# Converting the first two w_out tiles into a pool that opens with the second half of the attention

## The chip, the cores and the metric

The kernel runs on one core of a Trainium2 chip. The metric is the device time of one execution in microseconds (us); three executions of the kernel before took 803.8, 806.29 and 808.18 us, so the median is 806.29 us.

## What is computed

Attention for 4 batches, 8 heads, 576 positions and 64 dimensions, with a bias from a small network of relative positions, and behind it an MLP with a squared ReLU on the 2304 tokens:

```python
def _attn_ref(q, k, v, w1, b1, w2):
    ...
    h = np.maximum(x @ w1 + b1, 0.0)
    bias = h @ w2
    scores = scores + bias.transpose(2, 0, 1)[None, :, :, :]
    scores = scores - np.max(scores, axis=-1, keepdims=True)
    attn = np.exp(scores)
    attn = attn / (np.sum(attn, axis=-1, keepdims=True) + 1e-09)
    return np.matmul(attn, v).astype(np.float32)

def _moe_ref(x, w_in, w_out):       # x: 2304 x 512, w_in: 512 x 2048, w_out: 2048 x 512
    h = x @ w_in
    r = np.maximum(h, 0.0)
    g = r * r
    return (g @ w_out).astype(np.float32)
```

## The kernel before, in words

**Stages.** The attention runs in 80 units (batch, pair of heads, chunk of 128 rows), numbered `s` in the loop at L615; the second half, of batches 2 and 3, begins at `s == NA` = 40. There the pool `pre` opens on the left side of SBUF (L620). The MLP comes behind it: it runs over `items` (L684), each one block of tokens `n` and one pair `P` of 128-wide slices of the hidden layer. `up(i)` (L691) makes the products with w_in: 24 matmuls into the PSUM tile `ha`, 18 into `hb` (L704), then scales and combines them on ACT (L718), POOL (L719, L720) and DVE (L722, L723), squares them, and splits the result into a high part `gh` (ACT, L733) and a low part `gl` (DVE, L734). `down(i)` (L737) makes 24 matmuls with w_out (L753), for the item before. There is one `ha` and one `hb`, so the next item's `hb` matmuls wait until L722 and L723 have read the last ones.

**Weights.** Both weight matrices arrive as 64-bit floats and are cut into 32 tiles; tile `n` belongs to w_out where `n // 2` is odd (2, 3, 6, 7, 10, ...). A tile is loaded by one 512 KB transfer on SP into a buffer of the tag `stage` (L172), of which there are two. `lead_w` (L175) puts the 32-bit float together: one pass on ACT (L180) and four on DVE (L183 to L186). For w_out, `split_out` (L242) then writes the high part on ACT (L246) and the low part on POOL (L247) into the tile that the matmuls read. For w_in, `split_in` adds sums on POOL (L238 to L240) and ends with L227 on ACT and L228 on DVE. "A conversion" below is all of this for one tile. The scratch tile `wa` of a w_out conversion has two buffers, and each is free only when L247 has run.

**Order of the work.** Tiles of w_in up to 21 are converted during the attention, one in every second unit (`early`, `when`, L611 to L613). The remaining 20 tiles are in the list `todo` (L790); `convert(k)` takes the next `k` of them, with two loads ahead. `convert(C0)` takes two before the first item, and `convert(WC[i])` (L824) takes `WC[i]` between `up(i)` and `down(i - 1)`. A scheduler in the framework then sets the order on each engine from its own model of times, so instructions of the MLP can stand among those of the attention if their data and memory allow it. The tiles that the matmuls of w_out read lie in the pool `mlp` on the right side, in the place where the pools `att` and `kqb` of the attention were; `pre` holds `stage`, `wa` and `zw`.

**Stage buffers at item 3.** The outputs of `down(3)` are partial sums: each of four tiles `o` takes a `stage` buffer (L759), is copied from PSUM by ACT (L769) or DVE (L767), and is stored to DRAM (L772). They take their turn in the same two buffers as the weight loads.

Of the kernel before, what the change touches and what calls it, by code (L numbers as in the profile page):

```python
# [11 lines left out]
F32R = mybir.dt.float32r  # L12
# [23 lines left out]
WB, WS, LW, XS, XB, LAG, NE, SC, SN, AH = 40, 3, 4, 48, 70, 1, 13, 22, 16, 2  # L36
# [9 lines left out]
LW = 2  # L46
# [33 lines left out]
def attention_then_relu2_mlp(ctx: ExitStack, tc: tile.TileContext, q, k, v, cols, w_in, w_out, psi, xmat, dist, out):  # L80
# [47 lines left out]
    NU = len(units)  # L128
# [6 lines left out]
    def load_k(b, hp):  # L135
        t = kq_p[-1].tile([128, KO], F32, name="k1", tag="k1")
        SP.dma_start(out=t[0:64, :S], in_=k[b, hp, :, :S])
        SP.dma_start(out=t[64:128], in_=k[b, hp, :, S:])
        k1_t[b, hp] = t

    def load_v(b, hp):
        t = att.tile([128, 5, 2, D], F32, name="v", tag="v", bufs=AB * HP)
        SP.dma_start(out=t, in_=v[b, hp])
        v_t[b, hp] = t

    def load_q(b, hp):
        t = kq_p[-1].tile([128, S], F32, name="q1", tag="q1")
        for h in range(2):
            rows = slice(64 * h, 64 * h + 64)
            SP.dma_start(out=t[rows, 512:], in_=q[b, hp, TAIL, :, h, rows])  # L150
            SP.dma_start(out=t[rows, :512].rearrange("d (i m) -> d i m", i=TAIL), in_=q[b, hp, :TAIL, :, h].rearrange("i d m -> d i m"))
        q_t[b, hp] = t
# [16 lines left out]
    def load_w(n):  # L169
        t = stage_p["p"].tile([128, 2, 256, 2], I32, name="stage", tag="stage", bufs=2)  # L170
        src = (w_in, w_out)[n // 2 % 2][n // 4 * 2 + n % 2]
        SP.dma_start(out=t.rearrange("p g n t -> p g (n t)"), in_=src.bitcast(I32).rearrange("p (g n) -> p g n", g=2))  # L172
        wraw_t[n] = t

    def lead_w(n, a):  # L175

        raw = wraw_t.pop(n)
        low, high = (raw[:, :, :, t] for t in range(2))
        af = a.bitcast(F32)
        ins = ACT.activation(out=af, in_=high.bitcast(F32), func=AF.Abs)  # L180
        if n in early:
            tc.keep_in_program_order(ins)
        DVE.tensor_scalar(out=af, in0=af, scalar1=HI_MIN, scalar2=HI_MAX, op0=ALU.max, op1=ALU.min)  # L183
        DVE.tensor_scalar(out=a, in0=a, scalar1=3, scalar2=0x3FFFFFFF, op0=ALU.logical_shift_left, op1=ALU.bitwise_and)
        DVE.scalar_tensor_tensor(out=a, in0=high, scalar=-0x40000000, in1=a, op0=ALU.bitwise_and, op1=ALU.bitwise_or)  # L185
        DVE.scalar_tensor_tensor(out=a.bitcast(U32), in0=low.bitcast(U32), scalar=29, in1=a.bitcast(U32), op0=ALU.logical_shift_right, op1=ALU.bitwise_or)  # L186
# [21 lines left out]
    def scan_w(k):  # L208
        tc.keep_in_program_order(largest(wraw_t.pop(ins[k])[:, :, :, 1].bitcast(F32), wcols[:, k:k + 1]))

    def scale_w(ps_col):
        m = column()
        mi = m.bitcast(I32)
        largest(wcols, m)
        DVE.tensor_scalar(out=m, in0=m, scalar1=HI_MIN, scalar2=HI_MAX, op0=ALU.max, op1=ALU.min)
        t = column()
        DVE.tensor_scalar(out=t.bitcast(I32), in0=mi, scalar1=3, scalar2=0x3FFFFFFF, op0=ALU.logical_shift_left, op1=ALU.bitwise_and)
        DVE.scalar_tensor_tensor(out=mi, in0=mi, scalar=0x40000000, in1=t.bitcast(I32), op0=ALU.bitwise_and, op1=ALU.bitwise_or)
        return power(m, ps_col)

    def split_in(n, dst):
        z = stage_p["p"].tile([128, 9, 128], F32, name="zw", tag="zw")
        lead_w(n, z[:, 0:4].rearrange("p (g a) b -> p g (a b)", g=2).bitcast(I32))
        left_sums(z)
        hi, lo = dst
        sig = wscale[0]
        ACT.activation(out=hi, in_=z[:, 2:9], func=AF.Identity, scale=sig)  # L227
        DVE.scalar_tensor_tensor(out=lo, in0=z[:, 2:9], scalar=sig, in1=hi, op0=ALU.mult, op1=ALU.subtract)  # L228
        w_t[n] = (hi, lo)
# [5 lines left out]
    def left_sums(z):  # L235

        tt = POOL.tensor_tensor
        tt(out=z[:, 4:6], in0=z[:, 0:2], in1=z[:, 2:4], op=ALU.subtract)  # L238
        tt(out=z[:, 6:8], in0=z[:, 1:3], in1=z[:, 2:4], op=ALU.add)
        tt(out=z[:, 8], in0=z[:, 0], in1=z[:, 3], op=ALU.add)  # L240

    def split_out(n, dst):  # L242
        a = stage_p["p"].tile([128, 2, 256], F32, name="wa", tag="wa", bufs=2)
        lead_w(n, a.bitcast(I32))
        hi, lo = (x.rearrange("p (g n) -> p g n", g=2) for x in dst)
        ACT.copy(hi, a)  # L246
        POOL.tensor_tensor(out=lo, in0=a, in1=hi.bitcast(F32), op=ALU.subtract)  # L247
        w_t[n] = dst

    def is_in(n):  # L250
        return n // 2 % 2 == 0
# [277 lines left out]
    todo = [(ic, jb) for ic in chunks for jb in range(NJB)]  # L529
# [32 lines left out]
    wdst, xsig, alpha_t = {}, {}, {}  # L562
# [3 lines left out]
    def take(x, o, n):  # L566
        o += 18 * S * x
        return area[:, o:o + n]

    NB, NP = B + 1, NF // 2  # L570
# [13 lines left out]
    for m in range(1, 8):  # L584
        t = take(1, 896 + 512 * (m - 1), 512).bitcast(F16).rearrange("p (x c t) -> p x c t", x=2, c=2)
# [25 lines left out]
    for m, n in enumerate(early):  # L611
        last = (896 * m + 895) // (9 * S) if m < 11 else 2
        when[n] = max(WB + WS * m, NA + (B - AB) * NIC * (last + 1))  # L613
    waiting = []
    for s in range(NU + TL + 1):  # L615
        if s == NA:
            prep_stack.close()
            kq_stack.close()
            kq_p.append(kq_stack.enter_context(tc.tile_pool(name="kqb", bufs=3, side="right", reuse_waits="tile")))
            pre = ctx.enter_context(tc.tile_pool(name="pre", bufs=1, side="left", reuse_waits="tile"))  # L620
            stage_p["p"] = pre
            xT.extend(pre.tile([128, HP, S], F32, name=f"xT{b}") for b in range(AB, B))
        for m, g in enumerate(groups[AB * HP:]):
            if s == max(first[g] - KL, NA):
                load_k(*g)
                load_q(*g)
            if s == max(first[g] - KL + TL + 1, NA - AB * HP + 2 + TL + m):
                load_v(*g)
        if s == SC - 1:
            load_w(ins[0])  # L630
            load_w(ins[1])
        for n in early:
            if when[n] == s + LW:
                load_w(n)
        if s < NU:
            scores(s)
        if SC <= s < SC + SN:
            for m in range(NF * (s - SC) // SN, NF * (s - SC + 1) // SN):
                scan_w(m)
                if m + 2 < NF:  # L640
                    load_w(ins[m + 2])
        if s == SC + SN:
            pw = ps.tile([128, 512], F32, name="pw", tag="aux", bufs=4)
            wscale = scale_w(pw[:, 0:1])
        for n in early:
            if when[n] == s:
                split_in(n, wdst[n])
        if s == XS:
            pw = ps.tile([128, 512], F32, name="pw", tag="aux", bufs=4)
            set_scale(0, x_largest(0), pw[:, 0:1])  # L650
        if s == XB:
            split_x(0)
        if s < AB * HP * TAIL:
            n, r = divmod(s, AB * HP)
            bias_upto(NJB * (n + 1) + BO[r])
            if r == 4 and n + 2 < NIC:
                load_xc(chunks[n + 2])
        if 0 <= s - TL < NU:
            transposes(s - TL)
        if 0 <= s - TL - 1 < NU:  # L660
            values(s - TL - 1)
            b, hp, ic = units[s - TL - 1]
            if s - TL - 1 == NU - 1 or units[s - TL][:2] != (b, hp) and (b >= AB or ic == chunks[-1]):
                waiting.append((b, hp, normalise(b, hp)))
            elif waiting:
                scale_x(*waiting.pop(0))
        while waiting and s == NU + TL:
            scale_x(*waiting.pop(0))
# [108 lines left out]
                SP.dma_start(out=tails, in_=o)  # L777

    for n in range(4 * NP):
        if not is_in(n) and n < 4 * NP - 2:  # L780
            t = mlp.tile([128, 2, 512], F32R, name=f"w{n}")
            wdst[n] = (t[:, 0], t[:, 1])

# [6 lines left out]
    todo = [4 * P + 2 + f for P in range(NP // 2) for f in range(2)]  # L790
    for P in range(NP // 2, NP):
        todo += [n for n in range(4 * P, 4 * P + 4) if n not in early]
    done = loaded = 0
    def convert(k):
        nonlocal done, loaded
# [12 lines left out]
    for i in range(len(items) + LAG):  # L808
        if i == NP // 2:
            tmp_stack.close()  # L810
            late = ctx.enter_context(tc.tile_pool(name="late", bufs=1, side="right", reuse_waits="tile"))
            for n in (4 * NP - 2, 4 * NP - 1):
                t = late.tile([128, 2, 512], F32R, name=f"w{n}")
                wdst[n] = (t[:, 0], t[:, 1])
        if i < len(items):
            n, P = items[i]
# [60 lines left out]
```

## Time and profile before

| what | value |
|---|---|
| median of three executions | 806.29 us (803.8 to 808.18) |
| profiled execution, its time | 803.41 us |
| its span, first to last instruction | 801.6 us |
| granted TensorE clock, mean | 0.967 |
| busy PE, DVE, ACT, POOL | 731.9, 546.0, 453.8, 272.8 us |
| attention | 0 to about 402 us |
| MLP | about 402 us to the end |

The span leaves out what lies before the first and behind the last instruction (1.8 us here). Engines named: PE does matmuls, ACT, DVE and POOL work on vectors, SP issues the transfers. Times of rows are us from the start of the span, and `[2.16 <-DVE xT L723]` in a row says that the engine was idle for 2.16 us before it, and what ended that. [...]

### The profile page before, as it was taken

How to read it: one execution, taken by the hardware profiler on the slowest of the kernel's cores; microseconds unless marked ns; L12 is line 12 of the kernel's file. 1: busy time of each engine (PE TensorE's matmuls, PEld its weight loads, DVE VectorE, ACT ScalarE, POOL GpSimd, SP SyncE). 2: the span in 40 equal slices, each digit the busy share in tenths (PEclk: the TensorE clock that was granted, in tenths of full speed). 3: DMA queues.
4: the chain of work that ended last, by engine and by line, in shares of the span. 5: the costliest groups of instructions: out<-in, count | busy, mean ns of one | idle time of the engine just before them, and what ended most of it. 6: DMA issues, size and time to landing. Idle time of an engine off the chain costs nothing.

```text
span 801.6 us, 17870 instructions
## 1 busy us (share of the span) xinstructions
PE 731.9 (91%) x7238; PEld 583.4 (73%) x7238; DVE 546.0 (68%) x1135; ACT 453.8 (57%) x924; POOL 272.8 (34%) x292
## 2 busy tenths in 40 slices
PE   6499999999988898988999899989999999999992
PEld 5457787777766676666678677767888888888881
DVE  7877888875457778887888968785654466445541
ACT  5767787777645468786865555575642233224320
POOL 1454323340001012141266645745451244223320
PEclk7979999999999999999999999999999999999997
DMA  7610000000475422211221132102020001000100
GB/s 207 188 57 17 3 16 3 2 3 5 125 276 196 159 81 88 84 54 54 80 90 70 66 119 104 55 1 79 1 79 1 1 1 54 1 1 2 53 2 26
DMA packets 27990, 50.14 MB, mean 63 GB/s; under 512 B 5252, under 2 KB 13444, under 8 KB 27908
## 3 DMA queue, kind: packets, MB, share of 16 engines
q1 hardware_dynamic: 27908, 49.01, 18.6%
q8 instruction: 57, 0.93, 0.5%
q14 instruction: 25, 0.20, 0.1%
HBM read 43.23 MB, written 5.77 MB: 61 GB/s over the span
## 4 chain that ended last, share of the span: by engine, by line
PE 53%; DVE 17%; ACT 8%; DMA 7%; issue 7%; POOL 4%; SPq 2%; POOLq 0%; DVEq 0%; ACTq 0%
PE y L753 16%; PE sp L428 8%; PE px L495 7%; PE ha L704 7%; PE hb L704 6%; PE pp L477 5%; DMA stage<-in_w_in 4%; PE bb L383 4%; DVE t L434 2%; ACT p L439 2%; DVE area L605 2%; ACT pt L478 1%; DVE zw L185 1%; DVE area L228 1%; DVE small L189 1%
## 5 line engine op out<-in xcount | busy, mean ns | idle before, releaser
L753 PE MATMUL y<-w,gh 128*128 128x512 f32 x576 | 176.7, 401 | 2.6 <-ACT gh L733 2.4
L704 PEld LDWEIGHTS <-area 128*128 128x128 f16 x1680 | 148.1, 99 | 42.2 <-issue 17.6
L439 ACT ACTIVATE p<-t,negm 128x576 f32<-128x576 f32 x144 | 111.4, 776 | 27.3 <-DVE negm L434 27.1
L434 DVE CUSTOM_DVE_ANT_0 t<-sp,area 128x576 f32<-128x576 f32 x144 | 104.0, 753 | 29.9 <-PE sp L428 24.8
L753 PEld LDWEIGHTS y<-w,gh 128*128 128x128 f32 x576 | 105.1, 190 | 23.9 <-ACT gh L733 3.8
L428 PE MATMUL sp<-k,q 64*128 64x288 f32 (+1 forms) x640 | 105.3, 441 | 15.4 <-DVE negm L434 7.6
L495 PE MATMUL px<-pt,v 128*64 128x128 f32 (+1 forms) x1600 | 99.2, 272 | 7.5 <-DVE xT L500 2.8
L753 PE MATMUL y<-w,gl 128*128 128x512 f32 x288 | 106.0, 395 | 0.0
L704 PE MATMUL ha<-area 128*128 128x256 f16 (+1 forms) x960 | 105.2, 263 | 0.5 <-DVE xT L466 0.5
L478 ACT COPY pt<-pp 128x512 f32<-128x512 f32 x144 | 80.4, 583 | 41.5 <-PE pp L477 41.4
L495 PEld LDWEIGHTS px<-pt,v 128*64 128x64 f32 x1600 | 81.5, 139 | 24.2 <-issue 9.5
L704 PE MATMUL hb<-area 128*128 128x256 f16 (+1 forms) x720 | 83.9, 270 | 8.0 <-DVE area L723 4.7
L477 PE MATMUL pp<-ident,p 128*128 128x128 f32 x576 | 84.7, 283 | 3.3 <-ACT p L439 2.5
L428 PEld LDWEIGHTS sp<-k,q 64*128 64x128 f32 (+1 forms) x640 | 55.2, 179 | 39.7 <-issue 14.0
L398 POOL TENSOR_TENSOR area<-bt,bt 128x256 f32<-128x256 f32 x72 | 53.5, 768 | 80.6 <-DVE bt L393 80.6
L477 PEld LDWEIGHTS pp<-ident,p 128*128 128x128 f32 x576 | 62.2, 142 | 21.3 <-issue 8.4
L383 PE MATMUL bb<-wmov,mask 128*128 128x64 f16 x1440 | 51.2, 197 | 13.7 <-DVE bt L404 11.0
L753 PEld LDWEIGHTS y<-w,gl 128*128 128x128 f32 x288 | 53.7, 188 | 11.9 <-DVE gl L734 0.7
L383 PEld LDWEIGHTS <-mask 128*128 128x128 f16 x1440 | 46.9, 100 | 20.7 <-DVE bt L404 11.8
L719 POOL TENSOR_TENSOR area<-area 128x512 f32<-128x512 f32 (+1 forms) x20 | 24.3, 1215 | 92.8 <-ACT area L718 83.9
L369 DVE TENSOR_TENSOR mask<-sdist,theta 128x1024 f16<-128x1024 f16 (+1 forms) x78 | 50.3, 677 | 7.9 <-PE bb L383 7.9
L733 ACT CAST gh<-area 128x512 fp32r<-128x512 f32 (+1 forms) x40 | 22.2, 574 | 44.0 <-DVE area L728 32.9
(146 smaller groups left out, 1024.2 us busy)
## 6 DMA issues: line engine op xcount, KB each, us to landing
stage<-in_w_in SPq DMA_DIRECT2D x32, 512.0 KB, 3.7
stage<-in_w_out SPq DMA_DIRECT2D x16, 512.0 KB, 3.5
v<-in_v SPq DMA_DIRECT2D x16, 320.0 KB, 3.7
out<-o SPq DMA_DIRECT2D x18, 256.0 KB, 2.0
q<-in_q SPq DMA_DIRECT2D x32, 128.0 KB, 2.9
k<-in_k SPq DMA_DIRECT2D x16, 160.0 KB, 3.5
k<-in_k SPq DMA_DIRECT2D x16, 144.0 KB, 3.5
xc<-in_xmat SPq DMA_DIRECT2D x5, 288.0 KB, 3.3
```

The costliest lines, as they stand in the source:

```text
L369: DVE.tensor_tensor(out=m[:, :, :w], in0=win, in1=th.to_broadcast([128, 8, w]), op=ALU.is_ge)
L383: PE.matmul(bb[:, 64 * (7 - r):64 * (8 - r)], lhsT=m[:, r], rhs=wmov[:, n], start=(n == 0), stop=(n == 1))
L398: POOL.tensor_tensor(out=dst, in0=tw, in1=sw, op=ALU.add)
L428: mm = PE.matmul(out_t[to, x, :HALF], lhsT=qt[rows, cols], rhs=kt[rows, k0:k0 + HALF], start=True, stop=True)
L434: DVE.tensor_tensor_reduce(out=t.rearrange("p (x n) -> p x n", x=2), in0=sp[:, :, :HALF], in1=bias.rearrange("p (x n) -> p x n", x=2), sca ...
L439: ACT.activation(out=p[:, S * n:S * n + S], in_=t, func=AF.Exp, bias=negm[:, n:n + 1], scale=-1.0, accum_out=sums[:, 2 * ic + n:2 * ic + n ...
L477: PE.transpose(pp[:, 128 * c:128 * c + 128], p[:, k0:k0 + 128], ident)
L478: ACT.copy(pt[:, 4 * h:4 * h + 4], pp.rearrange("p (c m) -> p c m", c=4))
L495: PE.matmul(px[64 * h:64 * h + 64, :w], lhsT=vt[:, c, h], rhs=src, start=(c == 0), stop=(c == 4))
L704: PE.matmul(h[:, s, :w], lhsT=a, rhs=x, start=(k == 0), stop=(k == 5))
L719: POOL.tensor_tensor(out=c[:, 2:4], in0=s[:, 1:3], in1=s[:, 0:4:3], op=ALU.subtract)
L753: PE.matmul(y, lhsT=a[:, slot, o:o + 128], rhs=x, start=((n, P) in firsts and f == 0 and m == 0), stop=((n, P) in lasts and f == 1 and m = ...
```

## The change

Tiles 2 and 3, the first two of w_out, get their destination in `pre` instead of `mlp`, and their loads and conversions are written into the loop over the attention's units: the loads at `s` = 75 and 77, the conversions at 77 and 79. They leave `todo`, so that `convert` begins with tile 6, and every later tile comes two places earlier in it; `C0` and `WC` stay.

```diff
@@ attention loop
+    first_out = {2: NU - 3, 3: NU - 1}
...
             stage_p["p"] = pre
+
+            for n in first_out:
+                t = pre.tile([128, 2, 512], F32R, name=f"w{n}")
+                wdst[n] = (t[:, 0], t[:, 1])
...
             if when[n] == s:
                 split_in(n, wdst[n])
+        for n, at in first_out.items():
+            if s == at - LW:
+                load_w(n)
+            if s == at:
+                split_out(n, wdst[n])
@@ MLP
-        if not is_in(n) and n < 4 * NP - 2:
+        if not is_in(n) and n < 4 * NP - 2 and n not in first_out:
             t = mlp.tile([128, 2, 512], F32R, name=f"w{n}")
...
+    todo = [n for n in todo if n not in first_out]
```

How the order of the instructions moves is shown at three places. Lines of the changed kernel are 10 higher in `up` and `down` (L722 is L732, L723 is L733, L734 is L744, L718 is L728, L767 is L777), and 0 in the helpers ahead of the attention loop.

**First place: ACT at the end of the attention.** `w` is the converted tile, `wa` its scratch, `pt` and `pp` the transposed probabilities, `zw` the scratch of a w_in tile. Before:

```order
L227 ACTIVATE area<-zw,small 128x896
L478 COPY pt<-pp 128x512
L481 COPY pt<-pa 128x128
L246 CAST w_6235<-wa 128x512
L246 CAST w_6236<-wa 128x512
L180 ACTIVATE wa<-stage 128x512 x2
L718 ACTIVATE s<-ha,small 128x1024
```

With the change:

```order
L227 ACTIVATE area<-zw,small 128x896
L180 ACTIVATE wa<-stage 128x512
L478 COPY pt<-pp 128x512
L481 COPY pt<-pa 128x128
L246 CAST w_4001<-wa 128x512
L180 ACTIVATE wa<-stage 128x512
L246 CAST w_6257<-wa 128x512
L180 ACTIVATE wa<-stage 128x512
L728 ACTIVATE s<-ha,small 128x1024
```

The L246 of tile 2 has gone 12 rows up, to right behind the L180 of the last w_in tile; tile 6's L180 now stands ahead of the last L478, and tile 10's L180 ahead of the first item's L728.

**Second place: DVE from the last L228 of the attention to the first item.** Up to this L228 the order on DVE is the same in both. `ra` and `rt` are the last sums of the attention, `xT` its output. Before:

```order
L228 SCALAR_TENSOR_TENSOR area<-zw,small,area 128x896
L500 COPY xT_4001<-px 128x128
L500 COPY xT_4001<-px 128x64
L466 TENSOR_TENSOR xT_4001<-xT_4001,ra 128x512
L466 TENSOR_TENSOR xT_4001<-xT_4001,rt 128x64
L189 TENSOR_REDUCE small<-xT_4001 128x1 x2
L189 TENSOR_REDUCE small<-small 128x1 x2
```

With the change:

```order
L228 SCALAR_TENSOR_TENSOR area<-zw,small,area 128x896
L183 TENSOR_SCALAR wa<-wa 128x512
L500 COPY xT_4003<-px 128x128
L184 TENSOR_SCALAR wa<-wa 128x512
L185 SCALAR_TENSOR_TENSOR wa<-stage,wa 128x512
L500 COPY xT_4003<-px 128x64
L186 SCALAR_TENSOR_TENSOR wa<-stage,wa 128x512
L466 TENSOR_TENSOR xT_4003<-xT_4003,ra 128x512
L466 TENSOR_TENSOR xT_4003<-xT_4003,rt 128x64
```

The four passes of tile 6 have moved ahead of L466. Behind them, the passes of tiles 7 and 10 both end ahead of the first L732 and L733; before, tiles 6 and 7 were there, and the last pass of tile 7 stood between the two.

**Third place: DVE at the end of item 4.** `gl` is the low part for `down(3)`; `xT` is here the scratch of item 4, and the `o` is the first of the two output tiles of item 3 that DVE copies. Before, the two L722 and L723 follow the passes of tile 18:

```order
L734 TENSOR_TENSOR gl<-area,gh 128x512
L605 SCALAR_TENSOR_TENSOR area<-area,small 128x512
L185 SCALAR_TENSOR_TENSOR wa<-stage,wa 128x512
L186 SCALAR_TENSOR_TENSOR wa<-stage,wa 128x512
L722 SCALAR_TENSOR_TENSOR xT_77<-hb,small,xT_77 128x2x256
L723 SCALAR_TENSOR_TENSOR xT_77<-hb,small,xT_77 128x2x256
```

With the change:

```order
L185 SCALAR_TENSOR_TENSOR wa<-stage,wa 128x512
L186 SCALAR_TENSOR_TENSOR wa<-stage,wa 128x512
L183 TENSOR_SCALAR wa<-wa 128x512
L184 TENSOR_SCALAR wa<-wa 128x512
L185 SCALAR_TENSOR_TENSOR wa<-stage,wa 128x512
L186 SCALAR_TENSOR_TENSOR wa<-stage,wa 128x512
L732 SCALAR_TENSOR_TENSOR xT_77<-hb,small,xT_77 128x2x256
L733 SCALAR_TENSOR_TENSOR xT_77<-hb,small,xT_77 128x2x256
L183 TENSOR_SCALAR zw<-zw 128x512
L184 TENSOR_SCALAR zw<-zw 128x512
L777 COPY o<-y_6449 128x512
L185 SCALAR_TENSOR_TENSOR zw<-stage,zw 128x512
```

A third conversion (tile 23, behind tiles 19 and 22) has come in between the split of the next block's tokens (L605) and item 4's L732, and the copy to `o` stands inside the conversion of tile 24. From there on the conversions run about one item ahead: none is left among the L605 of the next split, where before tiles 30 and 31 stood.

## Rows read from the trace of the kernel before

**Rows 1.** The page: busy tenths of PE in 40 slices of 20 us.

```profile
PE   6499999999988898988999899989999999999992
```

**Rows 2.** Busy time by stretch: stretch, its length, busy us of each engine, PEclk, DMA.

```profile
450.00:460.00 10.00, 7.98 (x60) 6.23 (x57) 9.79 (x10) 6.86 (x10) 7.88 (x6) 1.00 0.18 58
460.00:470.00 10.00, 7.92 (x44) 5.69 (x43) 7.33 (x10) 6.18 (x8) 4.16 (x3) 0.83 0.30 97
...
530.00:540.00 10.00, 7.34 (x48) 5.55 (x47) 9.97 (x13) 4.62 (x7) 5.10 (x4) 0.86 0.00 0
540.00:801.60 261.60, 246.51 (x1744) 204.65 (x1741) 127.63 (x192) 87.69 (x135) 88.69 (x78) 0.98 0.07 23
```

**Rows 3.** Order of time, PE, 445 to 545: start, us, engine, line, what, [idle].

```profile
452.88 2.14 PE L704 MATMUL hb<-area 128*128 128x256 f16 x18
459.59 0.73 PE L753 MATMUL y<-w,gh 128*128 128x512 f32 x2 [1.96 <-ACT gh L733]
462.41 3.66 PE L704 MATMUL hb<-area 128*128 128x256 f16 x18 [2.08 <-DVE area L723]
...
502.02 3.03 PE L704 MATMUL hb<-area 128*128 128x256 f16 x18 [2.16 <-DVE xT L723]
513.87 2.13 PE L704 MATMUL hb<-area 128*128 128x256 f16 x18
524.01 2.13 PE L704 MATMUL hb<-area 128*128 128x256 f16 x18
536.92 3.73 PE L704 MATMUL hb<-area 128*128 128x256 f16 x18 [2.66 <-DVE area L723]
```

**Rows 4.** Single lines, whole span: DVE passes of w_out conversions, ns min/median/max.

```profile
L183 DVE TENSOR_SCALAR wa<-wa x16: 411/429/1509, 388.2 to 534.6; 128x512 f32<-128x512 f32 x16
...
L184 DVE TENSOR_SCALAR wa<-wa x16: 415/427/1403, 388.7 to 537.3; 128x512 int32<-128x512 int32 x16
...
L185 DVE SCALAR_TENSOR_TENSOR wa<-stage,wa x16: 675/692/1799, 389.2 to 538.3; 128x512 int32<-128x512 int32 x16
...
L186 DVE SCALAR_TENSOR_TENSOR wa<-stage,wa x16: 673/689/1662, 391.0 to 539.0; 128x512 uint32<-128x512 uint32 x16
```

**Rows 5.** Order of time, SP: loads of tiles 2 and 6.

```profile
382.98 0.33 SPq L172 DMA_DIRECT2D stage<-in_w_out  x1
...
395.95 0.33 SPq L172 DMA_DIRECT2D stage<-in_w_out  x1
```

**Rows 6.** Order of time, all engines, end of the attention and first items.

```profile
399.82 1.15 DVE L228 SCALAR_TENSOR_TENSOR area<-zw,small,area 128x896 f16<-128x896 f32 x1
...
399.95 1.18 ACT L246 CAST w<-wa 128x512 fp32r<-128x512 f32 x2
...
402.13 0.67 ACT L180 ACTIVATE wa<-stage 128x512 f32<-128x512 f32 x1 [1.01 <-POOL w L247]
...
402.54 0.21 DVE L466 TENSOR_TENSOR xT<-xT,rt 128x64 f32<-128x64 f32 x1
...
402.68 2.78 PE L704 MATMUL ha<-area 128*128 128x256 f16 x24 [0.51 <-DVE xT L466]
...
410.10 0.74 DVE L723 SCALAR_TENSOR_TENSOR c<-hb,small,c 128x512 f32<-128x512 f32 x1
```

**Rows 7.** Order of time, DVE at item 4.

```profile
452.07 0.75 DVE L723 SCALAR_TENSOR_TENSOR xT<-hb,small,xT 128x512 f32<-128x512 f32 x1
452.74 1.32 DVE L183 TENSOR_SCALAR wa<-wa 128x512 f32<-128x512 f32 x1
...
457.19 0.69 DVE L186 SCALAR_TENSOR_TENSOR wa<-stage,wa 128x512 uint32<-128x512 uint32 x1
```

**Rows 8.** Chain that ended last, in order of time: stores of item 3's outputs.

```profile
465.62 2.35 DMA py<-o
...
468.37 4.21 DMA py<-o
```

**Rows 9.** The page: issues, us to landing.

```profile
stage<-in_w_out SPq DMA_DIRECT2D x16, 512.0 KB, 3.5
```

## The prediction

> **What bounds the kernel now.** I read the page first: PE is busy for 9 tenths or more in most slices, and from slice 28 on in all but the last [rows 1]. So PE's work sets the time, and the question for any edit is where PE stands still. The view of busy time by stretch answers it [rows 2]: from 540 us to the end PE works 246.5 of 261.6 us, and most of the rest is the tail behind the last matmul. Between 450 and 540 there are stretches of 10 us in which it works 7.3 to 8.0, and there DVE is busy for up to 9.97. [...] The order of time on PE shows the places [rows 3]. Three times the 18 `hb` matmuls wait for a DVE instruction, L723, of the item before (2.08, 2.16 and 2.66 us), once the `y` matmuls wait for ACT (1.96 us). Behind such a stop the same 18 matmuls take 3.66, 3.03 and 3.73 us where they otherwise take 2.13.
>
> What it costs is read from the same rows. Two undisturbed `hb` groups start 513.87 and 524.01, so an item takes 10.14 us. From item 5's `hb` (452.88) to item 12's (536.92) there are 7 items in 84.04 us, where 7 x 10.14 = 71.0 would do: 13.1 us lost. Item 12's slow group adds 3.73 - 2.13 = 1.6. Together **14.7 us** can be had from this region, no more. What holds L723 back is DVE's fixed order: weight conversions stand ahead of it, one of them four passes of 2.24 us by the medians (429 + 427 + 692 + 689 ns), 2.2 by the smallest and 6.4 by the largest values [rows 4].
>
> **The change, part by part.**
>
> *What moves at all.* No instruction is added or removed. The loads of tiles 2 and 3 stand where they stood on SP: tile 2's was issued at 382.98, inside the attention, already in the kernel before [rows 5], and their DVE passes have kept their places too. What was late was the last step: both L246 ran at 399.95, since their destination lay in the attention's memory, and tile 6's L180, whose load was issued at 395.95, came only at 402.13, after a wait for a `wa` buffer that L247 had to free [rows 5, 6]. With a destination in `pre`, tile 2's L246 and L247 can run at about 392, so tile 6 starts some 2.5 us earlier, and by the order everything behind it moves forward: one conversion more is done by item 0, three more by item 4, and none is left in the split ahead of item 12.
>
> *The attention.* Tile 2's L246 (0.6 us on ACT) now stands ahead of an L478 that PE's transposed data pass through. PE has the next scores to do meanwhile, and the scores wait for DVE anyway; I cost it at nothing. Without this cover it would be 0.6 us. POOL's L247 goes into a gap in which POOL waited for DVE, with nothing queued behind it.
>
> *The start of the MLP.* DVE's last L228 ends at 399.82 + 1.15 = 400.97. Now tile 6's passes follow before L466, which releases the first `ha` matmul (402.68, behind L466's end at 402.75 by the modelled times) [rows 6]. That is 2.2 us more. Tile 10's load waits for tile 6's buffer, free at about 403.8, and lands 3.5 us later [rows 9]; its passes come behind tile 7's, from about 408.5 to 410.7, and L722 and L723 add 1.5: 412.2, against 410.10 + 0.74 = 410.84 before. So item 1 is late by **+1.5 us**. The ends: 0, if the passes fit into the wait for PE's last sums, and 3.7, if all 2.2 stays and the stop lowers the clock as at 462 (3.66 - 2.13 = 1.5).
>
> *Item 4.* Before, L723 ended at 452.82 and `hb` started at 452.88 [rows 3, 7]: no slack at all. A third conversion now stands ahead of it. Its price lies between 2.2 and 6.4 us [rows 4]; the nearest row is the next conversion at this very place, which took from 452.74 to 457.88, 5.1 us [rows 7]. I take 3.7, halfway from the median to that, since in it three passes of four were slow. DVE and PE are both late by the start's 1.5, so all of it becomes a stop, and I add 1.5 for the clock: **+5.2 us**, ends 2.2 and 7.9.
>
> *The outputs of item 3.* DVE's copy to the second `o` now stands inside tile 24's conversion, and by the buffers' turn it must wait until the first `o` is stored; the last copy waits for the second store. A store took 2.35 us, and 4.21 where the chain waited for the last [rows 8]. L722, L723 of item 5 and item 4's `gl` are queued behind. On SP the loads of tiles 23 and 24 now stand ahead of the four stores; tile 24's waits for tile 22's last pass, which is done before the first `o` is copied, so it holds none of them up. PE has `hb`, `ha` and half of `y` to do meanwhile, some 6 us. I take **+2.0**, ends 0 and 4.2.
>
> *Items 6 to 8.* Tiles 25 and 26 load only when those stores are done, as tiles 23 and 24 did before, and tile 25's passes stand ahead of a `gl`. I take **+1.0**, ends 0 and one load's 3.5 [rows 9].
>
> *What goes.* The stops at 459.59, 462.41 and 502.02 belong to pairs of conversions ahead of L722 that are now done earlier; the one at 536.92 belonged to tiles 30 and 31 among the passes of the split, and nothing of them is left there. I count all 14.7 us as gone, and what comes late instead as the four terms above. From 540 us on the two orders do the same work with PE full: nothing.
>
> *Sum:* -14.7 + 1.5 + 5.2 + 2.0 + 1.0 = **-5.0 us**. Against the profiled execution's 803.4 that is 798.4. The median of the runs is 2.9 above that execution, and I give the time against it: 806.3 - 5.0 = **801.3 us**. With all terms at their low ends it is -14.7 + 2.2 = -12.5 (793.8), at their high ends -14.7 + 19.3 = +4.6 (810.9).
>
> [...] The passes of one form take 675 to 1799 ns [rows 4], and at item 4 they are slow one after the other [rows 7] while POOL works. [...]
>
> **The rivals.**
>
> *Stops only change place* (no change). For it: DVE and POOL do the same work in 402 to 540, DVE was busy 9.79 and 9.97 of 10 us at two of the stops [rows 2], and a third conversion stands where there was no slack. Against it: the last conversions leave the split, where no new work takes their place. If the new terms reach 14 instead of 9.7, it ends at 805.6.
>
> *The change does not do what it says* (no change). The loads and the passes were in the attention before; one L246 and one L247 move, and the rest is the scheduler's order. Then the gain is one conversion's share of one stop, 2.2 us: 804.1. Against it: the order itself has moved by one item from item 4 on.
>
> *Every stop goes* (faster by more). If POOL happens to be quiet at item 4 and the stores land in 2.35 us, only 2.2 us comes back: 793.8. Against it: no conversion in this place took under 5 us.
>
> [...]
>
> **How the numbers follow.** About 0.5% of the median, 4 us, is what a measurement of this kernel can tell from no change. The forecast (801.3) gets 0.42, every stop gone 0.10: faster 0.52. Stops in other places get 0.18 and the change that does little 0.15: same 0.33. The slower rival gets 0.15. The range runs from 795 to 810: the bounds of the unknown terms, less the far ends of the first and last case, which leaves under 2 in 10 outside. The forecast's own case spans 798 to 802.3.
>
> **What would show it.** Right: no `hb` wait near item 12 and 10.1 us an item from about item 9 on; the first `ha` near 404.8; a stop of 3 to 5 us on L733 (L723 before) ahead of item 5's `hb`; DVE idle ahead of its copies to `o`, ended by a store. Wrong: tile 2's L246 still near 400, item 5's `hb` without a stop, or stops of over 2 us ahead of items 7 to 9, which I cost at 1 us in all. If the stretch from the first `ha` to item 12's `hb` is not shorter than 134.2 us, the forecast has failed.

## The result and the profile after: slower by 0.9%

The changed kernel takes 813.49 us (median of 12 executions, 809.27 to 816.44) against 806.28 us for the kernel before on the same chip (12, 803.21 to 809.62). The ratio is 1.0086, 95% interval 1.006 to 1.0112: **7 us slower**, where 5 us faster was forecast, with a range up to 810. The profiled execution took 811.21 us, its span is 809.4 us, the mean granted clock 0.965.

In the changed kernel's rows line numbers from the attention's loop on are ten higher: L704 is L714, L722 and L723 are L732 and L733, L733 and L734 are L743 and L744, L718 and L719 are L728 and L729 (five higher in E4, E6 and E7 below). Its page, busy time and PE's slices of 20 us:

```profile
PE 733.9 (91%) x7238; PEld 586.5 (72%) x7238; DVE 544.7 (67%) x1135; ACT 453.5 (56%) x924; POOL 269.5 (33%) x292
...
PE   5599999999988898988889698999999999999992
```

The work is the same as before (PE 731.9 us then). Against [rows 1] the slice from 440 to 460 us has fallen from 8 tenths to 6. The lengths by stage say more. Busy time by stretch, changed kernel: 386 to the first `ha`, to item 3's `hb`, to item 5's, to item 12's, to the end (length, then busy us of PE, PEld, DVE, ACT, POOL, then PEclk, the granted TensorE clock; in the kernel before it is 1.00 from 513.87 to 516.00, where the 18 `hb` take 2.13 us, and 0.50 from 463 to 465, inside the group that takes 3.66):

```profile
386.00:406.13 20.13, 16.19 (x197) 12.33 (x193) 18.30 (x42) 15.52 (x35) 5.30 (x7) 1.00 0.29 100
406.13:435.98 29.85, 28.25 (x198) 22.97 (x198) 26.33 (x39) 17.94 (x25) 18.28 (x13) 1.00 0.31 106
435.98:465.90 29.92, 21.38 (x137) 16.78 (x134) 26.42 (x33) 15.44 (x23) 18.03 (x13) 1.00 0.17 53
465.90:546.26 80.36, 76.33 (x463) 61.31 (x463) 58.12 (x72) 46.25 (x61) 47.15 (x37) 0.94 0.17 60
546.26:809.40 263.14, 248.09 (x1760) 206.71 (x1757) 126.46 (x192) 88.30 (x135) 83.93 (x74) 0.98 0.06 23
```

The same stretches of the kernel before:

```profile
386.00:402.68 16.68, 14.75 (x188) 11.51 (x186) 15.37 (x39) 13.31 (x29) 4.39 (x6) 1.00 0.28 95
402.68:431.84 29.16, 27.89 (x198) 22.96 (x198) 23.99 (x37) 17.85 (x25) 19.11 (x14) 1.00 0.25 91
431.84:452.88 21.04, 20.97 (x137) 16.67 (x134) 20.08 (x28) 12.67 (x19) 14.22 (x10) 1.00 0.10 31
452.88:536.92 84.04, 75.15 (x463) 59.69 (x463) 66.11 (x81) 48.08 (x64) 46.71 (x36) 0.96 0.22 75
536.92:801.60 264.68, 249.59 (x1758) 206.91 (x1758) 130.68 (x196) 90.77 (x138) 90.25 (x78) 0.97 0.06 23
```

Three things are to be seen. From item 3's `hb` to item 5's, 21.04 us without idle time on PE have become 29.92 with 8.5 idle: **+8.9**. Behind item 5 the change does gain, but only 3.7 + 1.5 = 5.2 us. And the first `ha` comes late; 1.2 us of that first stretch is how this execution stood at 386, so the table below counts from the last scores' pass on DVE (the last L434, start 395.79 before, 397.02 after) to the first `ha`: 6.89 before, 9.11 after, **+2.2**. Together, with 0.7 from the first `ha` to item 3's `hb`, it is 2.2 + 0.7 + 8.9 - 5.2 = 6.6 us, against 7.2 between the medians.

The stops themselves, order of time on PE, changed kernel (start, us, what, idle before and what ended it):

```profile
406.13 2.78 PE L714 MATMUL ha<-area 128*128 128x256 f16 x24 [2.16 <-DVE xT L466]
...
435.98 2.13 PE L714 MATMUL hb<-area 128*128 128x256 f16 x18
...
445.58 2.14 PE L714 MATMUL ha<-area 128*128 128x256 f16 x18 [1.65 <-DVE area L605]
448.59 0.71 PE L714 MATMUL ha<-area 128*128 128x256 f16 x5 [0.87 <-DVE area L605]
...
451.44 1.36 PE L714 MATMUL hb<-area 128*128 128x256 f16 x11 [2.00 <-DVE area L605]
...
465.90 3.35 PE L714 MATMUL hb<-area 128*128 128x256 f16 x18 [3.49 <-DVE xT L733]
...
504.88 3.78 PE L763 MATMUL y<-w,gh 128*128 128x512 f32 x8 [2.97 <-ACT gh L743]
516.01 2.13 PE L714 MATMUL hb<-area 128*128 128x256 f16 x18
...
536.17 2.13 PE L714 MATMUL hb<-area 128*128 128x256 f16 x18
```

Of the stops of [rows 3] none stands where it stood: those of 459.59, 462.41, 502.02 and 536.92 are gone, and items 9 to 12 run at 10.1 us each. In their place item 4 waits three times for L605, the split of the next block of tokens, item 5 for L733, and the `y` of item 7 for ACT. Why the split is late, order of time around item 3 (DVE's rows, with ACT's and POOL's between them, others left out):

```profile
433.04 0.42 DVE L183 TENSOR_SCALAR wa<-wa 128x512 f32<-128x512 f32 x1
...
433.95 1.74 DVE L185 SCALAR_TENSOR_TENSOR wa<-stage,wa 128x512 int32<-128x512 int32 x1
435.62 1.75 DVE L744 TENSOR_TENSOR gl<-c,gh 128x512 fp32r<-128x512 f32 x1
437.29 0.68 DVE L186 SCALAR_TENSOR_TENSOR wa<-stage,wa 128x512 uint32<-128x512 uint32 x1
438.00 0.62 ACT L246 CAST w<-wa 128x512 fp32r<-128x512 f32 x1 [3.71 <-DVE wa L186]
...
438.70 1.29 POOL L247 TENSOR_TENSOR w<-wa,w 128x512 fp32r<-128x512 f32 x1 [1.88 <-ACT w L246]
...
439.05 1.11 ACT L728 ACTIVATE area<-ha,small 128x1024 f32<-128x1024 f32 x1
...
440.07 1.61 POOL L602 TENSOR_TENSOR xs<-xT 128x512 f32<-128x512 f32 x1
...
441.65 1.29 POOL L729 TENSOR_TENSOR area<-area 128x512 f32<-128x512 f32 x1
...
442.97 0.75 DVE L732 SCALAR_TENSOR_TENSOR area<-hb,small,area 128x512 f32<-128x512 f32 x1 [1.92 <-POOL area L729]
...
444.79 0.73 DVE L605 SCALAR_TENSOR_TENSOR area<-xT,small,area 128x512 f16<-128x512 f32 x1
...
464.31 0.74 DVE L732 SCALAR_TENSOR_TENSOR xT<-hb,small,xT 128x512 f32<-128x512 f32 x1
```

The two rows of the kernel before that they are compared with, the split's first L605 and item 4's L722:

```profile
436.26 0.75 DVE L605 SCALAR_TENSOR_TENSOR area<-xT,small,area 128x512 f16<-128x512 f32 x1
...
451.29 0.74 DVE L722 SCALAR_TENSOR_TENSOR xT<-hb,small,xT 128x512 f32<-128x512 f32 x1
```

Tile 18, which the list now gives to item 2, is converted from 433.04 to 437.97. Two engines stand in order behind it. ACT's L246 waits 3.71 us for the last pass, and item 3's own L728 comes behind that. POOL's L247 waits for that L246, an L602 runs behind it until 441.68, and item 3's L729 only then, though L728 had ended at 440.16. DVE's L732 waits 1.92 us for L729, and the split stands behind L732 and L733. So the split's first L605 starts 8.81 us behind item 3's `hb` (444.79 - 435.98); before it was 4.42 (436.26 - 431.84). That is **4.4** of the 8.9. From there to item 4's L732 it is 19.5 us (464.31 - 444.79), before 15.0 (451.29 - 436.26): one more conversion among the same work, **4.5**, of which tile 23's own four passes are 3.2.

### The profile page after: what moved, and what is told of

It is laid out like the page before. It is cut to its first block, busy times and chain, and to the rows that moved or that the text cites. A ratio compares the mean times of both kernels' runs of the same rounds, so it can differ in the third digit from the quotient of the medians.

```text
span 809.4 us, 17870 instructions
## 1 busy us (share of the span) xinstructions
PE 733.9 (91%) x7238; PEld 586.5 (72%) x7238; DVE 544.7 (67%) x1135; ACT 453.5 (56%) x924; POOL 269.5 (33%) x292
## 4 chain that ended last, share of the span: by engine, by line
PE 57%; DVE 17%; issue 7%; ACT 6%; DMA 6%; POOL 3%; SPq 1%; POOLq 0%; DVEq 0%; ACTq 0%
PE y L763 17%; PE sp L428 8%; PE ha L714 8%; PE px L495 6%; PE hb L714 6%; PE pp L477 5%; PE bb L383 5%; DMA stage<-in_w_in 3%; DVE t L434 3%; DMA stage<-in_w_out 2%; ACT p L439 2%; DVE area L605 1%; PE ra L456 1%; ACT pt L478 1%; DVE small L189 1%
## 5 line engine op out<-in xcount | busy, mean ns | idle before, releaser
L714 PEld LDWEIGHTS <-area 128*128 128x128 f16 x1680 | 148.3, 99 | 44.0 <-issue 20.1
L434 DVE CUSTOM_DVE_ANT_0 t<-sp,area 128x576 f32<-128x576 f32 x144 | 103.9, 752 | 31.0 <-PE sp L428 25.9
L714 PE MATMUL ha<-area 128*128 128x256 f16 (+1 forms) x960 | 105.9, 265 | 4.7 <-DVE area L605 2.5
L478 ACT COPY pt<-pp 128x512 f32<-128x512 f32 x144 | 80.3, 582 | 39.6 <-PE pp L477 39.4
L714 PE MATMUL hb<-area 128*128 128x256 f16 (+1 forms) x720 | 80.9, 264 | 7.4 <-DVE xT L733 3.7
L729 POOL TENSOR_TENSOR area<-area 128x512 f32<-128x512 f32 (+1 forms) x20 | 24.3, 1214 | 93.8 <-ACT area L728 93.7
L729 POOL TENSOR_TENSOR xT<-xT 128x512 f32<-128x512 f32 (+1 forms) x18 | 22.9, 1272 | 70.7 <-ACT xT L728 70.0
```

Source lines behind the costliest of these rows:

```text
L434: DVE.tensor_tensor_reduce(out=t.rearrange("p (x n) -> p x n", x=2), in0=sp[:, :, :HALF], in1=bias.rearrange("p (x n) -> p x n", x=2), sca ...
L478: ACT.copy(pt[:, 4 * h:4 * h + 4], pp.rearrange("p (c m) -> p c m", c=4))
L714: PE.matmul(h[:, s, :w], lhsT=a, rhs=x, start=(k == 0), stop=(k == 5))
L729: POOL.tensor_tensor(out=c[:, 2:4], in0=s[:, 1:3], in1=s[:, 0:4:3], op=ALU.subtract)
```

## The experiments

The theory after reading this: the loss is the shift of the list, which brings tiles 18 and 23 ahead of steps of items 3 and 4 that DVE has no slack for. The rivals: the early work itself (its place in memory, its passes inside the attention), and passes that are long beside POOL's work (up to 1.80 us for a median of 0.69 [rows 4]), wherever they stand. Eleven kernels were run, one of them twice (E9 and E12). Each was also profiled, and its trace cut at the same four points; the last column is the sum, from the last L434 to the end, against before. Where two kernels have the same order the stretches mostly repeat to a few tenths (20.92 us in four of them), so they tell more than the spans. They do not always: E9 and E12 are one kernel, and their last two stretches differ by 0.8 and 1.2 us, their sums by 1.9, their ratios by 0.5%. So a difference of 2 us in one sum, or of 0.3% in one ratio, is little to rest on.

| kernel | ratio to before (95%) | median, us | L434 to `ha` | to item 3's `hb` | to item 5's | to the end | sum against before |
|---|---|---|---|---|---|---|---|
| before | 1 | 804.8 to 806.3 | 6.89 | 29.16 | 21.04 | 348.72 | 0 |
| changed | 1.0086 (1.006–1.0112) | 813.49 | 9.11 | 29.85 | 29.92 | 343.50 | +6.6 |
| E1 list back | 1.0049 (1.0031–1.0068) | 810.04 | 9.23 | 30.65 | 20.92 | 348.79 | +3.8 |
| E2 list forward | 1.0039 (1.0019–1.0059) | 809.25 | 6.89 | 29.58 | 30.97 | 343.30 | +4.9 |
| E4 places alone | 1.0049 (1.003–1.0068) | 809.21 | 9.11 | 30.53 | 20.92 | 349.01 | +3.8 |
| E5 done sooner | 1.0025 (1.0006–1.0045) | 806.68 | 6.89 | 29.07 | 21.14 | 350.95 | +2.2 |
| E6 place of tile 3 | 1.0022 (1.0004–1.004) | 807.05 | 6.89 | 30.75 | 21.46 | 349.01 | +2.3 |
| E7 place of tile 2 | 1.0052 (1.003–1.0074) | 809.71 | 9.11 | 30.49 | 20.92 | 348.99 | +3.7 |
| E8 pause at item 3 | 1.0072 (1.0047–1.0096) | 809.50 | 9.20 | 30.42 | 25.63 | 344.64 | +4.1 |
| E9 pause, none early | 1.0066 (1.0038–1.0094) | 809.51 | 6.89 | 29.63 | 27.53 | 342.78 | +1.0 |
| E12 the same again | 1.0018 (0.9994–1.0042) | 807.20 | 6.89 | 29.49 | 28.35 | 343.98 | +2.9 |
| E10 later, 1 1 2 2 | 0.9972 (0.9954–0.9991) | 803.96 | 6.89 | 29.48 | 20.93 | 347.64 | -0.9 |
| E11 later, 1 2 1 2 | 0.9969 (0.9952–0.9987) | 804.42 | 6.90 | 29.10 | 21.15 | 347.59 | -1.1 |
| E13 early and later | 1.0028 (1.0008–1.0049) | 807.75 | 9.11 | 30.91 | 20.92 | 347.79 | +2.9 |

(The expectations count from the last scores on PE, 2.4 us ahead of L434's start: their 9.3 and 11.5 are 6.9 and 9.1 here.)

**E1 and E2: the two halves of the change.** E1 is the changed kernel with

```diff
-C0 = 2
+C0 = 0
```

> The changed kernel with C0 = 0 for 2: the two tiles stay early, and every other conversion goes back to the item at which it stood before the change. Theory (the shift of the list costs it: tiles 18 and 23 stand on VectorE ahead of the split's and the combine's steps of items 3 and 4): the stretch from item 3's hb to item 5's hb is about 21 us again for 29.9, and the time is 803 to 807 us, what is left being the start of the MLP at most 2 us late less what no conversion ahead of item 0 saves. Rival 1 (the early work itself costs it, by its passes inside the attention and its place in memory): no better than 811 us. [...]

E2 is the kernel before with

```diff
-C0 = 2
+C0 = 4
```

> The kernel before with C0 = 4 for 2: no tile is early, but all four first conversions stand ahead of item 0, so from item 0 on the list is where the change puts it. Theory: item 3's hb to item 5's hb takes about 30 us as in the changed kernel, and the time is 811 to 815 us (with two more conversions ahead of item 0, maybe 1 to 3 us more). Rival 1 (the early work itself): 804 to 808 us, as before. [...]

Both lose. E2, without anything early, shows the stops of the changed kernel one by one. Order of time on PE in E2:

```profile
435.03 2.13 PE L704 MATMUL hb<-area 128*128 128x256 f16 x18
...
444.67 0.82 PE L704 MATMUL ha<-area 128*128 128x256 f16 x6 [1.07 <-DVE area L605]
...
451.55 2.38 PE L704 MATMUL hb<-area 128*128 128x256 f16 x11 [2.00 <-DVE area L605]
...
466.00 3.48 PE L704 MATMUL hb<-area 128*128 128x256 f16 x18 [2.65 <-DVE xT L723]
```

So the shift makes these stops (30.97 us from item 3's `hb` to item 5's, 30 expected). Its time, 809.25 us, is below the 811 to 815 that I gave, but the stops stand where the list puts them; the cost is 4.9 us by the trace, the gain behind item 5 included, and 3.2 by the ratio. E1 has these stretches back at 20.92 and 348.79, as expected, and still takes 4 us more than the kernel before, 3 more than the upper end I gave. The theory was half of it: the other half lies ahead of item 3. By the ratios the halves, 0.49% and 0.39%, add to the change's 0.86%; by the traces 3.8 and 4.9 come to 8.7 for 6.6, and those 2 us are not explained.

**E4: places alone.** The changed kernel without the early loads and conversions; only the two tiles' memory stays in `pre`:

```diff
-        for n, at in first_out.items():
-            if s == at - LW:
-                load_w(n)
-            if s == at:
-                split_out(n, wdst[n])
...
-    todo = [n for n in todo if n not in first_out]
```

> The changed kernel with only the places of the two tiles kept in the pool of the attention's second half; loads and conversions are where they were before the change. Theory: 805 to 808 us, no difference from before. Rival 1, in its form that the place in memory costs it: 810 us or more.

The theory missed: 809.21 us, between its 808 and the rival's 810, with E1's ratio, 1.0049, 9.11 us to the first `ha`, and 20.92 from item 3's `hb` to item 5's. The early code adds nothing that these runs show to what the free place does: before, too, the conversions of tiles 2 and 3 stood in the attention up to their last two steps [rows 5, 6]. What the place does is seen at the attention's end in the changed kernel, order of time (L246 and L247 of tiles 2 and 3, tile 6's passes and the last L466; others left out):

```profile
392.92 0.62 ACT L246 CAST w<-wa 128x512 fp32r<-128x512 f32 x1 [1.09 <-DVE wa L186]
...
393.62 1.27 POOL L247 TENSOR_TENSOR w<-wa,w 128x512 fp32r<-128x512 f32 x1 [7.49 <-ACT w L246]
...
402.12 0.42 DVE L183 TENSOR_SCALAR wa<-wa 128x512 f32<-128x512 f32 x1
...
402.69 1.51 POOL L247 TENSOR_TENSOR w<-wa,w 128x512 fp32r<-128x512 f32 x1 [3.04 <-ACT w L246]
403.11 1.64 DVE L185 SCALAR_TENSOR_TENSOR wa<-stage,wa 128x512 int32<-128x512 int32 x1
...
404.80 0.68 DVE L186 SCALAR_TENSOR_TENSOR wa<-stage,wa 128x512 uint32<-128x512 uint32 x1
...
405.40 0.68 DVE L466 TENSOR_TENSOR xT<-xT,ra 128x512 f32<-128x512 f32 x1
...
406.00 0.21 DVE L466 TENSOR_TENSOR xT<-xT,rt 128x64 f32<-128x64 f32 x1
```

Tile 2's buffer `wa` is free at 394.9 (393.62 + 1.27) instead of about 402 (tile 6's L180 came at 402.13 then, behind a wait for L247 [rows 6]), so tile 6, the next to use it, has its four passes on DVE from 402.12, ahead of the last two L466, on which the first `ha` waits. Before, they came behind those. Of the 2.2 us about 1 is that L185 took 1.64 us for its median of 0.69 [rows 4], beside tile 3's L247 on POOL; in E1 it is L184 (1.50 for 0.43), in E4 and E7 L185 again (1.64). No run has the passes here without that L247.

**E6 and E7: which place.** E4 with one place only, tile 3's (E6) or tile 2's (E7):

```diff
-    first_out = {2: NU - 3, 3: NU - 1}
+    first_out = {3: NU - 1}
...
+    first_out = {2: NU - 3}
```

> The kernel before with the place of tile 3 alone in the pool of the attention's second half. New theory of the early half of the loss: with its place free early, tile 2's last two steps (L246, L247) no longer wait for the attention's end, its buffer wa comes free early, and the four passes of the third tile (tile 6), which takes that buffer, run on VectorE ahead of the attention's last two L466, on which item 0's first product waits. Here tile 2's buffer stays held as before, so: last scores to first ha 9.3 us as before (not 11.5), and 804 to 807 us. Rival (any place in that pool costs it): 11.5 us and 808 to 810 us.

> The kernel before with the place of tile 2 alone in the pool of the attention's second half. Theory as for the kernel with tile 3's place: here tile 2's buffer comes free early and tile 6's passes stand ahead of the attention's last L466: last scores to first ha 11.5 us, and 807.5 to 810 us, as with both places. Rival (each place costs half): about 10.4 us and 807 us in both.

The two stand apart just so: 6.89 and 9.11 us. In E6 (first fence, DVE and PE) nothing stands ahead of L466 but the attention's own copies; in E7 (second fence) the four passes of tile 6 do:

```profile
404.68 0.59 DVE L500 COPY xT<-px 128x128 f32<-128x128 f32 x2
...
405.73 0.69 DVE L466 TENSOR_TENSOR xT<-xT,ra 128x512 f32<-128x512 f32 x1 [0.47 <-PE ra L456]
...
406.34 0.21 DVE L466 TENSOR_TENSOR xT<-xT,rt 128x64 f32<-128x64 f32 x1
406.48 2.78 PE L709 MATMUL ha<-area 128*128 128x256 f16 x24 [0.52 <-DVE xT L466]
```

```profile
402.89 0.42 DVE L183 TENSOR_SCALAR wa<-wa 128x512 f32<-128x512 f32 x1
...
403.88 1.64 DVE L185 SCALAR_TENSOR_TENSOR wa<-stage,wa 128x512 int32<-128x512 int32 x1
...
406.77 0.21 DVE L466 TENSOR_TENSOR xT<-xT,rt 128x64 f32<-128x64 f32 x1
...
406.90 3.30 PE L709 MATMUL ha<-area 128*128 128x256 f16 x15 [2.18 <-DVE xT L466]
```

That is shown, then, for the 2.2 us; E7's 809.71 us lies in the range that I gave. E6 took 807.05 us, just above the 807 I gave as the upper end: it has 1.6 us more in the next stretch, where the changed kernel has 0.7 and E1 and E4 1.4 to 1.5. By the order the same thing happens there with tile 7, which takes tile 3's buffer; no run takes that apart.

**E8 and E9 (again as E12): a pause ahead of the split.** The shift is kept up to tile 15 and taken back from tile 18 on, in the changed kernel (E8) and in E2 (E9, E12):

```diff
-WC = (1, 2, 2, 1, 2, 2, 1, 1, 1, 2, 1, 2, 1, 2, 1)
+WC = (1, 2, 1, 0, 2, 2, 1, 1, 1, 2, 1, 2, 1, 2, 1)
```

> The changed kernel, but with item 2 taking one conversion for two and item 3 none for one, so that tiles 18, 19 and all behind them stand where they stood before the change, and only tiles 6 to 15 stay two places earlier. Theory (it is tile 18 at item 2 and 19 at item 3, ahead of the split's and item 3's steps on VectorE, that cost the shift): item 3's hb to item 5's hb is 21 us or less (29.9 in the changed kernel), and the stops before item 5's y and item 6's hb (4 us together before) shrink since VectorE comes to them earlier; the early half stays (11.5 us from last scores to first ha): 804 to 809 us. [...]

> The kernel before with four conversions ahead of item 0 for two, item 2 taking one for two and item 3 none for one: as the kernel with the pause at item 3, without anything early. Theory: no early half (9.3 us from last scores to first ha), item 3's hb to item 5's hb 21 us or less, smaller stops at items 5 and 6: 800 to 805 us. Rival (passes slow wherever they stand): 808 to 811 us, as with the list moved forward alone.

> The same kernel as the one with the pause at item 3 and nothing early, for a narrower time. From its trace (last scores to the end 409.2 us against 408.2 us before) the time should be 805 to 808 us; if it is 809 us or more again, something ahead of the last scores, where both kernels have the same order, costs it.

All three stretches missed: 25.63 us in E8, 27.53 and 28.35 in E9 and E12, where I expected 21 or less, and the times lie above what I gave for E8 (809.50 for 804 to 809) and E9 (809.51 for 800 to 805). One part came: in E8 the split's L605 starts 4.85 us behind item 3's `hb` (442.08 - 437.23), so tile 18 was what held it up. But item 5's `hb` then waits 4.49 us for L733, with two passes of a conversion still ahead of it. What is saved behind item 5 (344.64 for 348.72) pays for it, no more. E9's time rested on 6 executions and E8's on 5; E12, the same kernel as E9 with 12, is at 1.0018, in the 805 to 808 us that E9's trace asked for. I count the pause as no gain over the kernel before, and take nothing else from E9's and E8's times.

**E5: the gain alone, and E10 and E11: the list moved back.** E5 has the kernel before finish its list at item 10, as the changed kernel does, without moving anything ahead of item 7:

```diff
-WC = (1, 2, 2, 1, 2, 2, 1, 1, 1, 2, 1, 2, 1, 2, 1)
+WC = (1, 2, 2, 1, 2, 2, 1, 2, 2, 2, 1, 1, 1, 2, 1)
```

> The kernel before with one conversion more at items 7 and 8 and fewer at item 11 (the table's places 7 and 8 are 2 for 1, places 10 and 11 are 1... that is, the last conversion stands at item 10, not item 11): the one thing that the change gained, alone. Theory (the stop of about 4.3 us ahead of item 12's hb comes of two conversions beside the split at item 11): that stop goes, 801 to 804 us, unless the conversions moved to items 7 and 8 give it back there, as they did in the changed kernel at item 8: then 805 to 807 us. Rival (that stop is slack for something later): 806 us.

The stop of 2.66 us ahead of item 12's `hb` shrinks to 0.73, but the `y` of item 10 now waits 1.12 and 0.65 us, and a part of that `hb` another 1.33 for the split: from item 11's `hb` to item 12's it is 14.93 us (12.91 before), and from item 5's `hb` to the end 350.95 for 348.72. The time, 806.68 us, is the 805 to 807 that I gave for this case. The stops of [rows 3] are not slack that lies about; an earlier conversion moves them. So the other way, E10 (first) and E11 (second):

```diff
-WC = (1, 2, 2, 1, 2, 2, 1, 1, 1, 2, 1, 2, 1, 2, 1)
+WC = (1, 2, 2, 1, 1, 1, 2, 2, 1, 2, 1, 2, 1, 2, 1)
...
+WC = (1, 2, 2, 1, 1, 2, 1, 2, 1, 2, 1, 2, 1, 2, 1)
```

> The kernel before with the conversions at items 4, 5, 6, 7 counted 1, 1, 2, 2 for 2, 2, 1, 1: tiles 19, 22, 23 and 24 come an item or more later, none earlier. Theory (VectorE is the bound up to item 6 and has room behind it, so a conversion that is moved back, not forward, pays): the stops before item 5's y and item 6's hb (4 us and a slow clock behind them) go or shrink, item 3's hb to item 5's hb stays at 21 us, and item 5's hb to the end is 344 to 348 us for 348.7: 800 to 805 us. Rival (the place on VectorE is not it; the total work is): 804 to 807 us, the stops come back at items 7 to 9.

> The kernel before with the conversions at items 4, 5, 6, 7 counted 1, 2, 1, 2 for 2, 2, 1, 1: a half dose of the kernel with 1, 1, 2, 2. Theory: item 5's hb to the end 345 to 349 us, 801 to 806 us. Rival: 804 to 807 us.

Both took less than the kernel before, by 2.3 and 2.5 us by the ratios and 0.9 and 1.1 by the traces. That is less than their theory's middle, and E11's 804.42 us lies in its rival's range too. Busy time by stretch of E10, item 5's `hb` to item 12's:

```profile
457.56:540.50 82.94, 73.19 (x463) 58.36 (x463) 61.68 (x81) 47.42 (x64) 45.98 (x36) 1.00 0.22 77
```

PE idles a little longer there than before (82.94 - 73.19 = 9.75 us, before 84.04 - 75.15 = 8.89), so the stops do come back, as the rival had it; what is gained is that its matmuls take 73.19 us at a clock of 1.00, for 75.15 at 0.96. E11 shows the same (73.19 us at 1.00), and in E13 the matmuls of this stretch take 73.27 us.

**E13: early and later.** The changed kernel with two edits:

```diff
-WC = (1, 2, 2, 1, 2, 2, 1, 1, 1, 2, 1, 2, 1, 2, 1)
+WC = (1, 2, 2, 1, 1, 2, 1, 2, 1, 2, 1, 2, 1, 2, 1)
...
-C0 = 2
+C0 = 0
```

> The changed kernel with C0 = 0 and items 4 to 7 counted 1, 2, 1, 2: the two tiles early, and the rest of the list where the half dose of the later list has it. If the two effects add (early places +4.0 us, later list -2.5 us): 806 to 809 us, with last scores to first ha 11.5 us, item 3's hb to item 5's hb 21 us, and item 5's hb to the end 347.6 us. If the early places only cost it while the list is early too: 803 to 805 us.

They add: 807.75 us and 1.0028, with the three stretches as forecast. No table of the list that was tried pays for the early places.

## Why the prediction was wrong, point by point

Two steps of the sum failed. The first is the -14.7 with only +2.0 and +1.0 against it: the stretch behind item 5 gained 5.2 us for the 11.7, since new stops took the place of the old ones. The second is item 4's +5.2: the path to item 5's `hb` lost 8.9 us, since tile 18 at item 2 holds up the split as well.

- **What goes, -14.7: the stops went, the time did not.** The named stops are gone, and items 9 to 12 run at 10.1 us, as I said. But the stretch from item 5's `hb` on gained only 5.2 us, since new stops stand in it. The rival "stops only change place", with 0.18, was the better case; its price for the new terms was too low, and it does not have to end at no change.
- **Item 4, +5.2: measured +8.9.** I found the stop at the right place and priced it about right: the third conversion cost 4.5 us (I had 3.7), and item 5's `hb` waited 3.49 us, within the 3 to 5 that I asked the trace to show, and ran 3.35 for 2.13, at a granted clock of 0.61 (these 1.2 us, which I had counted here, lie in the stretch behind). What I missed is that the same shift puts tile 18 at item 2, and that item 4's `ha` needs the next block's split. I priced the third conversion ahead of item 4 and did not ask what the two ahead of it were late for. The chain from tile 18's last pass over ACT (L246) and POOL (L247, L602, L729) to DVE (L732, L733, L605) follows the order of each engine.
- **Items 6 to 8, +1.0, and the outputs of item 3, +2.0.** The stores held up nearly nothing (DVE's first copy to `o` waited 0.47 us for one, the second not at all). What held things up stands on ACT: behind item 8's `hb` item 7's `y` waits 2.97 us for L743. ACT had waited 6.59 us for DVE's L733, and between L735 and L743 there are, beside its own L736, a wait of 0.92 us for a transfer, tile 30's L180 and a w_in tile's L227. So the load is a part of it, not all. Item 8 to item 9 takes 16.24 us for 10.1, **6.1** over, with the clock at 0.71 from 500 to 510; E2, with the same list and nothing early, has a stop of 2.96 us at this place. I had capped it at one load's 3.5 us and left out the slow clock behind such a stop, which I had counted at item 12. Order of time on ACT:

```profile
499.80 1.06 ACT L735 ACTIVATE area<-area 128x1024 f32<-128x1024 f32 x1 [6.59 <-DVE area L733]
501.78 0.66 ACT L180 ACTIVATE wa<-stage 128x512 f32<-128x512 f32 x1 [0.92 <-DMA stage<-in_w_out]
...
503.29 1.03 ACT L227 ACTIVATE area<-zw,small 128x896 f16<-128x896 f32 x1
504.23 1.12 ACT L743 CAST gh<-area 128x512 fp32r<-128x512 f32 x2
```

- **The start, +1.5: measured +2.9** (2.2 to the first `ha`, 0.7 to item 3's `hb`), within its ends. The mechanism, tile 6's passes ahead of L466, is what E6 and E7 show. My middle took it that the 2.2 would be made up in part by item 1; it was not. Its end with a slow clock did not come here: the first 24 `ha` took 2.78 us as before, at a granted clock of 1.00. In E7, E8 and E13 they took 4.28, 4.23 and 4.45 us.
- **The attention, nothing: not contradicted.** PE does wait 1.02 us for ACT's L478 at 394.08, as the order let one fear, and before a wait of 0.99 us for DVE stood at 393.40 in its stead. The last L434 starts 1.2 us later than before, but E9 and E12, one kernel, differ by 4.7 there.
- **The slower rival, 0.15,** had the right sign. Its price for item 4, 6.4 us for a conversion with every pass as long as the longest of [rows 4], no run shows: of the passes of conversions from item 3's `hb` to item 5's, 4 of 9 took over 1.2 us before, and 4 of 13 now. These 4 (L183 at 451.90, 1.50 us; L184 at 455.64, 1.51; L186 at 459.49, 1.64; L185 at 461.96, 1.71) each started while a POOL instruction ran and ended 0.28 or 0.55 us behind it. So did L185 at 403.11 (two inputs): it took 1.64 us and ended 0.55 behind POOL's L247, which ran from 402.69 to 404.20. L186 at 451.30 and L185 at 458.78, beside which POOL's L602 started later, took their usual 0.68. E1 and E2 show that the passes have to be moved for the loss at items 3 to 5. Long passes beside POOL are part of the loss: about 1 of the 2.2 us at the start, and beside tile 18, where POOL ran L247 (433.85, 1.30 us) and L602 (435.23, 1.59), L185 took 1.74 and L744 1.75 us. No run takes POOL away, so it is not shown that POOL makes them long, nor how much of the whole it would be.
- **The account.** Forecast against measured: start 1.5 and 2.9; item 4 5.2 and 8.9; everything behind item 5, -14.7 + 2.0 + 1.0 = -11.7 and -5.2. The misses add to 1.4 + 3.7 + 6.5 = 11.6 us, from -5.0 to +6.6.

My own test, that the stretch from the first `ha` to item 12's `hb` must be shorter than 134.2 us, failed: it is 546.26 - 406.13 = 140.1.

## What to carry to other kernels

Giving a tile its place earlier does not only start that tile's work earlier: it can free the buffer behind it (tile 2's place did, tile 3's alone did not at this point), and so pull the next user of that buffer forward, into the queue of an engine whose next result may be what everything waits for. If a list of side work is spread by a table of counts, taking its first entries away moves every later entry; look at each one for what it is now ahead of, and above all where an engine in order stands behind it (ACT here: its L246 waited 3.71 us for tile 18's last pass, with item 3's L728 behind). Here, too, earlier was not better: with two more tiles done throughout (E2) the kernel lost 3 us, with one or two fewer done by items 4 to 6 (E11, E10) it gained about 2. E10, which holds back more, gained no more than E11, so that later is always better is not shown.

## What the runs showed of the hardware

- **Behind stops of about the same length the clock fell or stayed.** Each stop of [rows 3] before an `hb`, 2.08 to 2.66 us, has a slow group behind it (granted clock over the three groups 0.57, 0.68 and 0.54; 1.00 over those of 513.87 and 524.01). E10 has as much idle time in the same items, its longest stops 1.46, 1.55 and 1.65 us, and its granted clock is 1.00 over the whole stretch. By the trace that is all of its gain. But length alone did not decide: ahead of the first `ha` the changed kernel, E4 and E1 stop for 2.16, 2.19 and 2.38 us, and the 24 `ha` behind take 2.78 us in all three (granted clock 1.00 in the changed kernel); E7, E13 and E8 stop for 2.18, 2.22 and 2.38, and there they take 4.28, 4.45 and 4.23.
- **Two passes with one tensor input were long beside POOL too.** In the changed kernel L183 at 451.90 took 1.50 us and L184 at 455.64 took 1.51, for a median of 0.43 [rows 4], while POOL ran L602 (451.46, 1.66 us) and L729 (455.02, 1.85 us). Both ended 0.28 us behind the POOL instruction; the three long ones with two inputs named above (L186 at 459.49, L185 at 461.96 and 403.11) ended 0.55 behind. No run here shows why.
- **Spans scatter ahead of the change.** E9 and E12 are one kernel; their last L434 starts at 400.37 and 395.69 us, and their spans are 807.2 and 804.4, though behind L434 the first is the shorter one (406.8 and 408.7). What makes the difference in the attention was not tried. Differences of a few us between two profiled spans say nothing by themselves; the same stretches of two traces say more, and even they differ by up to 1.2 us between these two.
